# Cluster labels from one product per tile, and an issue order from a stored list of shifts

## The chip, the cores and the metric

The kernel runs on one core of a Trainium2 chip. The core has five engines that work through instruction streams of their own: TensorE (PE in the profile; its weight loads are listed apart as PEld), VectorE (DVE), ScalarE (ACT), GpSimd (POOL) and SyncE (SP), which issues all DMAs here. Semaphores order the streams; within a stream, order is fixed when the program is built. The metric is device time in microseconds, the median over runs; lower is better.

## The reference

Clustered attention, then a feed-forward block. For 4 batches, 8 heads, 768 positions and 64 dimensions per head, every query and key is given the label of the one of its head's 16 centroids with the largest cosine, and a query attends only to keys with its own label:

```
q_assign = argmax(q_n . c_n)          # per head, 16 clusters
k_assign = argmax(k_n . c_n)
scores = where(q_assign == k_assign, q . k / 8, -1e9)
attn = softmax(scores);  x = attn @ v           # 3072 rows of 512
h = x @ w_in;  g = where(h >= 1, h, where(h <= -1, 0, (h + 1)^2 / 4))
out = g @ w_out                                  # 512 -> 2048 -> 512
```

## The kernel before, in words

Inputs are float32. Each operand of a product is split into two halves in half precision (hi and lo), and products are summed over the hi and lo terms that matter. The work is cut into 8 units (`NU`): batch b and chunk c, where a chunk is 2 of the 6 position tiles of 128 per head. Heads go in pairs (hp, 4 of them).

Per batch and head pair: `kv_load`, `k_scale` (a power-of-two scale), `k_split` (hi and lo, then a transpose by DMA into `kT`), `v_split`, and `k_assign` (labels of 12 key tiles, written as a one-hot mask beside the keys). Per unit: `q_load`, `q_scale`, `q_split`, `q_assign` (labels of 16 query tiles) and `q_pairs`. Then, per unit and head pair, 4 score tiles: `at_scores` multiplies (a *score group*: 4 products with 384 columns into a PSUM tile `pair`), and VectorE evicts it (an *eviction*: `CUSTOM_DVE_ANT_0 sS<-pair`, whose accumulator read writes `sbi`); `at_soft` takes the exponential on ScalarE, splits it with ScalarE and GpSimd and transposes it by DMA; `at_av` multiplies with v into `banka` (tiles `pT`, `rr`). After each unit, `ffn1` (24 products with 256 columns into one of the banks h, i, j; then `r` on VectorE, ScalarE, VectorE; `g` on ScalarE and GpSimd) and `ffn2` (12 products with 512 columns into `pair`) run once per 256 of the 2048 hidden columns. In the first steps the weights of the feed-forward block are also brought in and split (`w`, `wk`, `word`: VectorE, ScalarE and GpSimd).

**Labels.** `labels` multiplies each transposed tile `xT[:, i]` (its 128 contraction rows hold the hi and the lo half of the 64 dimensions) with `cT[:, a]`, the 16 centroids of its head: a = 0 holds the hi half of the centroids twice, a = 1 the lo half. The two products, each a weight load and a matmul with 16 columns, accumulate in PSUM to one z of 16 columns. VectorE then takes the maximum over 16 (`mx`), compares, multiplies with `iota`, and takes the maximum again.

**Order of issue.** Nothing is issued at once. A `Recorder` keeps every instruction as a node with its predecessors (products of one `rec.group()` are one node), and `issue` decides the order. `forward` is a list scheduler: it steps through a model of the engines (`Machine`, with prices from `price`, latencies, a throttled TensorE clock) and takes on each engine the ready node with the lowest priority value. `backward` does the same from the end and gives new priorities. `issue` alternates them 80 times (`ROUNDS`), replays each order by `replay` at 4 phases of the clock window with random delays, keeps the order with the lowest sum, and then emits it. All engines' streams follow that order, so every instruction stands at the recorder's one line, and groups are told apart by tile names.

`early()` is true for steps under 22 (the first unit and a half): there, score groups alternate between the two `pair` tiles. Later ones use `pair[0]` alone, and `pair[1]` belongs to `ffn2`.

Of the kernel before, what the change touches and what calls it, by code (L numbers as in the profile page):

```python
# [34 lines left out]
WINDOW, SLOW, FULL = 3413.0, 0.41, 0.77  # L35
PHASES = (0.0, 850.0, 1700.0, 2550.0)


LATER, LATER_DMA, SLACK = 25, 600, 20

# [3 lines left out]
LOOK, MARGIN = 0.4, 4000  # L44
ROUNDS = 80

class Recorder:
# [9 lines left out]
    def __init__(self, tc):  # L59
        self.tc, self.nc = tc, tc.nc  # L60
        self.nodes, self.seen, self.open, self.step = [], {}, None, -99
        for name in ("tensor", "scalar", "vector", "gpsimd", "sync"):
            setattr(self, name, Engine(self, name, getattr(tc.nc, name)))
# [23 lines left out]
    def price(self, eng, op, out, ins, kw):  # L87
# [11 lines left out]
        if eng == "tensor":  # L99
            n = self.free(ins[1])  # L100
            half = self.free(ins[0]) <= 64 and n > 100
            if ins[1].dtype == F32:
                n *= 4

            return n / 4.8 + 3.5 if half else max(n / 2.4 + 2.5, 24)
        if eng == "scalar":
# [24 lines left out]
    def add(self, eng, op, fn, args, kw):  # L131
        outs = [kw[k] for k in ("out", "accum_out") if kw.get(k) is not None]
        pos = [a for a in args if isinstance(a, bass.AP)]
        if "out" not in kw:
            outs.insert(0, pos.pop(0))
        ins = pos + [a for k, a in kw.items() if k not in ("out", "accum_out") and isinstance(a, bass.AP)]
        node = self.open
        if node is None:
            node = Node(eng, self.step, len(self.nodes))
            self.nodes.append(node)  # L140
# [42 lines left out]
    def forward(self, prio):  # L183
# [3 lines left out]
        at = dict.fromkeys(self.nodes, 0.0)  # L187
        m = Machine(PHASES[0], slack=SLACK)
        clock = m.clock
# [46 lines left out]

    def replay(self, phase):

        m = Machine(phase, Random(int(phase)))
        left = {x: len(x.preds) for x in self.nodes}  # L240
        at = dict.fromkeys(self.nodes, 0.0)
        todo = {}
        for x in reversed(self.order):
            todo.setdefault(x.eng, []).append(x)
        while todo:
            starts = []
            for e, q in todo.items():
                x = q[-1]
                if not left[x]:
                    t = max(m.clock.get(e, 0.0), at[x])  # L250
                    starts.append((max(t, m.free(x, t)), x.i))
            t, i = min(starts)
            x = self.nodes[i]
            todo[x.eng].pop()
            if not todo[x.eng]:
                del todo[x.eng]
            self.done(x, m.run(x, t), at, left, lambda y: None)
        return m.span

    def backward(self, prio):  # L260
# [42 lines left out]
        return start  # L303

    def issue(self):
        for x in self.nodes:
            for y in x.preds:
                y.succs.append(x)
        prio = {x: x.step for x in self.nodes}
        best = None  # L310
        for _ in range(ROUNDS):
            self.forward(prio)
            starts = {x: x.start for x in self.nodes}
            span = sum(self.replay(p) for p in PHASES)
            if best is None or span < best[0]:
                best = span, self.order
            prio = self.backward(starts)
        span, self.order = best
        with self.tc.manual_schedule():
            for x in self.order:  # L320
                for fn, args, kw in x.calls:
                    fn(*args, **kw)  # L322


class Machine:


    def __init__(self, phase, noise=None, slack=0):
        self.noise, self.slack = noise and noise.random, slack
        self.clock, self.bank = {}, {}  # L330
# [15 lines left out]
    def run(self, x, t):  # L346

        e = x.eng
        if x.dma:
# [8 lines left out]
            end = self.ring + (490 if tr else 1300)  # L358
            if self.noise:
                end += LATER_DMA * self.noise()  # L360
            self.sent.append(end)
        else:
# [3 lines left out]
            end = x.busy + LATENCY[e] + self.slack  # L366
            if self.noise:
                end += LATER * self.noise()
        for k in x.banks:
# [18 lines left out]
class Node:  # L388
    def __init__(self, eng, step, i):
        self.eng, self.step, self.i = eng, step, i  # L390
        self.banks = set()
# [4 lines left out]
class Group:  # L396
# [5 lines left out]
    def __enter__(self):  # L402
        r = self.rec
        r.open = Node("tensor", r.step, len(r.nodes))
        r.nodes.append(r.open)

    def __exit__(self, *a):
        self.rec.open = None

# [38 lines left out]
def tile_clustered_attention_moe(  # L448
# [203 lines left out]

    def labels(z1, xT, n, heads):

        with rec.group():
            for i in range(n):
                for a in range(2):
                    h = heads[i]
                    rec.tensor.matmul(
                        z1[:, i], xT[:, i], cT[:, a, h * C : (h + 1) * C], start=(a == 0), stop=(a == 1)  # L660
                    )
# [9 lines left out]
        return wide(mx)  # L671

# [49 lines left out]
    def k_assign(b, hp):  # L722

        e = KV[b, hp]
        n = 2 * T
        z1 = misc(n, C)
# [540 lines left out]
    for s in sorted(ev):  # L1267
        rec.step = s
        for fn, args in ev[s]:
            fn(*args)  # L1270
    rec.issue()
# [32 lines left out]
```

## Time and profile before

| | |
|---|---|
| median of 3 runs | 867.04 us (865.24 to 868.20) |
| profiled execution, own time | 869.13 us |
| its span, first to last instruction | 867.3 us |
| TensorE busy | 809.4 us, 93% |
| VectorE busy | 650.4 us, 75% |
| ScalarE busy | 637.4 us, 73% |
| GpSimd busy | 550.1 us, 63% |
| mean granted TensorE clock | 0.984 |

The page gives each engine's busy time, the chain of work that ended last, and groups of like instructions (busy time, mean duration, idle time before them and what ended it). A matmul's duration is its whole way through the array; the next one starts long before that ends. The pace of TensorE is therefore read from starts: from the start of one group to the start of the next, divided by the number of products.

### The profile page before, as it was taken

To read this page: it belongs to the slowest core of one execution; us is meant where nothing else is said; L and a number is where in the kernel's file an instruction comes from. 1 tells how busy PE (TensorE), PEld (TensorE's weight loads), DVE (VectorE), ACT (ScalarE), POOL (GpSimd) and SP (SyncE) were. 2 spreads that over 40 slices of the span, in tenths; PEclk is the share of its full clock that TensorE was granted. 3 is DMA by queue.
4 is the path that set the end of the run, shared out by engine and by line. 5 is a ranking of instruction groups with operands and counts; after the bars stand their busy time and mean duration, and the time that the engine had idled before them with its cause. 6 is when DMAs were issued, how large, how long until landed. Compare 5 with 4: busy or idle time off the path is not lost.

```text
span 867.3 us, 19633 instructions
## 1 busy us (share of the span) xinstructions
PE 809.4 (93%) x7452; PEld 561.1 (65%) x7452; DVE 650.4 (75%) x1485; ACT 637.4 (73%) x1128; POOL 550.1 (63%) x527
## 2 busy tenths in 40 slices
PE   3687559999999999999999999999999999999997
PEld 3454346666767766767666766767667667676664
DVE  7999999998978868678778768678887757544322
ACT  6799888986867778678777687686776687676232
POOL 1166688876756777756766677666667577666222
PEclk9998889999999999999999999999999999999999
DMA  9985689869999979988998978998999787666100
GB/s 315 241 248 146 171 204 204 147 140 162 197 169 199 168 151 177 192 185 190 183 189 173 169 141 173 198 161 167 177 216 162 141 160 131 113 135 109 20 25 25
DMA packets 404767, 142.55 MB, mean 164 GB/s; under 512 B 372800, under 2 KB 396352, under 8 KB 404672
## 3 DMA queue, kind: packets, MB, share of 16 engines
q1 hardware_dynamic: 404672, 141.30, 80.2%
q8 instruction: 58, 0.95, 0.5%
q14 instruction: 37, 0.30, 0.1%
HBM read 40.40 MB, written 6.29 MB: 54 GB/s over the span
## 4 chain that ended last, share of the span: by engine, by line
PE 80%; DVE 12%; ACT 3%; issue 2%; DMA 2%; POOL 0%; ACTq 0%; SPq 0%; DVEq 0%; POOLq 0%
PE pair L322 40%; PE banka L322 11%; PE bankj L322 10%; PE banki L322 9%; PE bankh L322 9%; DVE sS L322 2%; DVE w L322 2%; DVE wk L322 1%; ACT w L322 1%; DMA q<-qn 1%; ACT hl L322 1%; DVE banki L322 1%; DVE qn L322 1%; ACT sS L322 1%; DVE q L322 1%
## 5 line engine op out<-in xcount | busy, mean ns | idle before, releaser
L322 POOL TENSOR_TENSOR hl<-sS,hl 128x768 f16<-128x768 f32 x176 | 299.8, 1711 | 116.0 <-ACT hl L322 83.7
L322 PE MATMUL pair<-w,g 128*128 128x512 f16 x1152 | 271.1, 379 | 0.0
L322 PEld LDWEIGHTS <-w 128*128 128x128 f16 x2304 | 223.4, 98 | 44.3 <-issue 2.6
L322 ACT ACTIVATE sS<-sS,sbi 128x768 f32<-128x768 f32 x192 | 179.3, 934 | 91.9 <-DVE sbi L322 88.6
L322 DVE CUSTOM_DVE_ANT_0 sS<-pair,zero,er 128x768 f32<-128x768 f32 x192 | 194.2, 1011 | 66.4 <-PE pair L322 41.6
L322 PEld LDWEIGHTS <-g 128*128 128x128 f16 x1152 | 110.3, 98 | 116.3 <-issue 1.6
L322 PE MATMUL pair<-kv,q 128*128 128x384 f16 x768 | 160.9, 334 | 17.6 <-DVE sbi L322 9.2
L322 ACT CAST hl<-sS 128x768 f16<-128x768 f32 x176 | 143.8, 825 | 12.9 <-DMA pT<-hl 7.9
L322 POOL TENSOR_TENSOR g<-r,g 128x512 f16<-128x512 f32 x88 | 103.7, 1179 | 63.7 <-ACT g L322 53.8
L322 PEld LDWEIGHTS <-q 128*128 128x128 f16 x1152 | 84.1, 99 | 72.8 <-issue 26.1
L322 PE MATMUL banka<-pT,kv 128*64 128x256 f16 (+1 forms) x1680 | 107.2, 282 | 0.4 <-DMA pT<-hl 0.4
L322 ACT ACTIVATE r<-r,f_ra,f_rs 128x512 f32<-128x512 f32 x88 | 71.3, 811 | 43.3 <-DVE r L322 42.5
L322 PEld LDWEIGHTS <-kv 128*64 128x64 f16 (+1 forms) x1968 | 96.9, 108 | 2.9 <-issue 1.5
L322 ACT CAST g<-r 128x512 f16<-128x512 f32 x88 | 53.8, 611 | 13.1 <-DVE r L322 10.2
L322 PE MATMUL bankh<-x,w 128*128 128x256 f16 x432 | 51.9, 273 | 0.2 <-POOL x L322 0.2
L322 POOL TENSOR_TENSOR qn<-qn,phi 128x256 f16<-128x256 f16 x48 | 34.2, 731 | 27.1 <-DVE phi L322 17.5
L322 PE MATMUL bankj<-x,w 128*128 128x256 f16 x408 | 48.3, 273 | 0.0
L322 PE MATMUL banki<-x,w 128*128 128x256 f16 x312 | 38.0, 273 | 0.0
L322 POOL TENSOR_TENSOR w<-w 128x1024 f16<-128x1024 f32 x12 | 30.2, 2513 | 10.6 <-ACT w L322 9.3
L322 PE MATMUL banki<-wk,w 128*128 128x256 f16 x312 | 36.7, 273 | 0.0
L322 ACT ACTIVATION_READ_ACCUMULATOR sS<-sS,sbi 128x1 f32 x192 | 36.0, 188 | 0.0
L322 PEld LDWEIGHTS <-ones 128*128 128x128 bf16 x256 | 18.0, 105 | 27.2 <-issue 21.6
(238 smaller groups left out, 1069.0 us busy)
## 6 DMA issues: line engine op xcount, KB each, us to landing
w<-in_moe_w_out_dram SPq DMA_DIRECT2D x14, 512.0 KB, 4.4
q<-in_q_dram SPq DMA_DIRECT2D x12, 512.0 KB, 4.9
kv<-in_k_dram SPq DMA_DIRECT2D x16, 384.0 KB, 3.8
kv<-in_v_dram SPq DMA_DIRECT2D x16, 384.0 KB, 4.4
out_dram<-o SPq DMA_DIRECT2D x11, 512.0 KB, 3.3
w<-in_moe_w_in_dram SPq DMA_DIRECT2D x10, 512.0 KB, 5.6
word<-in_moe_w_in_dram SPq DMA_DIRECT2D x6, 512.0 KB, 4.6
o<-in_v_dram SPq DMA_DIRECT2D x8, 384.0 KB, 4.5
```

Of the source, the lines that this page charges most:

```text
L322: fn(*args, **kw)
```

## The change

Three things change.

1. `labels`: outside `early()`, one product per tile with both halves of the centroids, `cT[:, :, h*C:(h+1)*C]`, 32 columns, into a PSUM tile twice as wide. A new `tensor_reduce` on VectorE adds the two halves into a tile in SBUF: for queries `zs`, for keys the third part of the slot, where the raw v lay. The first maximum and the comparison read that tile; the rest is as it was. Early label groups (4 of 16 for keys, 2 of 12 for queries) are unchanged.
2. Prices in `price` for products with at most 64 output rows: 3.5 ns less each, and 248 ns (`TILED`) for each group that has any; the least price of a product is 25.2 instead of 24.
3. `issue`: 59 rounds of `forward` and `backward` without `replay`; then 200 stored seeds each shift the priorities of a few recorded steps (`nudge`), and one last `forward` gives the order.

The core of the diff (the list of 200 seeds and the removed `replay` left out):

```diff
+PHASE = 0.0
...
+BASE = 59
+NUDGES = (
+    1700000017, 1700000018, 1700000028, 1700000071, 1700000073, 1700000079, 1700000104, 1700000109,
...
+)
+TILED = 248
...
-            return n / 4.8 + 3.5 if half else max(n / 2.4 + 2.5, 24)
+            self.tiled |= half
+            return n / 4.8 if half else max(n / 2.4 + 2.5, 25.2)
...
+    def nudge(self, seed, prio):
+
+        a = mix(seed * 2654435761 + 1)
+        b = mix(a + 1)
+        c = mix(b + 1)
+        names = sorted({x.ev for x in self.nodes})
+        lo, every, size = b % len(names), (1, 2, 5)[(a >> 8) % 3], float(500 << ((a >> 16) % 5))
+        at = {y: i for i, y in enumerate(names)}
+        for x in self.nodes:
+            i = at[x.ev]
+            if lo <= i < lo + (1 << (a % 8)) and not (i - lo) % every:
+                r = c if c >> 8 & 1 else mix(c + i * 7919)
+                prio[x] += ((r & 0xFFFF) / 32768.0 - 1.0) * size
...
         prio = {x: x.step for x in self.nodes}
-        best = None
-        for _ in range(ROUNDS):
+        for _ in range(BASE):
             self.forward(prio)
-            starts = {x: x.start for x in self.nodes}
-            span = sum(self.replay(p) for p in PHASES)
-            if best is None or span < best[0]:
-                best = span, self.order
-            prio = self.backward(starts)
-        span, self.order = best
+            prio = self.backward({x: x.start for x in self.nodes})
+        for seed in NUDGES:
+            self.nudge(seed, prio)
+        self.forward(prio)
...
-    def labels(z1, xT, n, heads):
-
+    def labels(xT, n, heads, tmp):
+
+        both = not early()
+        z1 = misc(n, 1 + both, C)
         with rec.group():
             for i in range(n):
+                h = heads[i]
+                if both:
+                    rec.tensor.matmul(z1[:, i], xT[:, i], cT[:, :, h * C : (h + 1) * C], start=True, stop=True)
+                    continue
...
+        zz, z1 = z1, z1[:, :, 0]
+        z = tmp if both else z1
+        if both:
+            rec.vector.tensor_reduce(out=z, in_=zz.rearrange("p n a c -> p n c a"), op=ALU.add, axis=AX.X)
...
-        rec.vector.tensor_reduce(out=mx, in_=z1, op=ALU.max, axis=AX.X)
-        rec.vector.tensor_tensor(out=z1, in0=z1, in1=wide(mx), op=ALU.is_equal)
+        rec.vector.tensor_reduce(out=mx, in_=z, op=ALU.max, axis=AX.X)
+        rec.vector.tensor_tensor(out=z1, in0=z, in1=wide(mx), op=ALU.is_equal)
...
-        mx = labels(z1, e["kT"], n, [2 * hp + i // T for i in range(n)])
+        z1, mx = labels(e["kT"], n, [2 * hp + i // T for i in range(n)], view(e["parts"][2], [n, C], F32))
...
-        z1 = misc(NQ, C)
-        mx = labels(z1, e["qT"], NQ, [i // CT for i in range(NQ)])
         zs = e["z"] = new("zs", [NQ, C], F32)
+        z1, mx = labels(e["qT"], NQ, [i // CT for i in range(NQ)], zs)
```

What it moves. On TensorE, 14,586 rows become 13,978: 608 fewer, 304 weight loads and 304 matmuls. The streams of all engines are rearranged from about the first score group on. Three places follow, in the order of the program.

VectorE, from the eviction of the 21st score group on (the rows `ISA sS_..,sbi_..` are evictions and their accumulator reads; `r` belongs to `ffn1`, `hl` to `v_split`, `word` and `wk` to the weights, `aq`'s `bankj`, `iq` and `sq` to `q_scale`), before:

```order
L322 ISA sS_85,sbi_156<-pair_79,zero,er_148 128x768
L322 ISA sbi_156 128x1
L322 SCALAR_TENSOR_TENSOR r_209<-bankj,f_gs_204,r_209 128x512
L322 SCALAR_TENSOR_TENSOR hl_172<-kv_62,sv_141,hl_172 128x768
L322 SCALAR_TENSOR_TENSOR word_71<-word_71,wk_69 128x1024
L322 ISA sS_86,sbi_157<-pair_80,zero,er_148 128x768
L322 ISA sbi_157 128x1
L322 TENSOR_SCALAR bankj<-bankj 128x4
L322 RECIPROCAL rs_160<-rs_160 128x4
L322 TENSOR_SCALAR iq_127<-bankj 128x4
L322 RECIPROCAL sq_129<-iq_127 128x4
L322 SCALAR_TENSOR_TENSOR word_71<-word_71 128x1024
```

and now, from the same eviction on:

```order
L350 ISA sS_85,sbi_156<-pair_79,zero,er_148 128x768
L350 ISA sbi_156 128x1
L350 ISA sS_86,sbi_157<-pair_80,zero,er_148 128x768
L350 ISA sbi_157 128x1
L350 TENSOR_SCALAR r_209<-bankj,f_lo_184,f_hi_179 128x512
L350 TENSOR_REDUCE v_am_125<-x_74 128x1
L350 SCALAR_TENSOR_TENSOR r_209<-bankj,f_gs_204,r_209 128x512
L350 TENSOR_SCALAR wk_69<-wk_69 128x1024
L350 TENSOR_SCALAR bankj<-bankj 128x4
L350 TENSOR_SCALAR iq_127<-bankj 128x4
L350 RECIPROCAL sq_129<-iq_127 128x4
L350 SCALAR_TENSOR_TENSOR word_71<-word_71,wk_69 128x1024
```

The row behind each piece is the eviction of the 23rd group. Before, three long operations stand between the evictions of the 21st and 22nd group and one between those of the 22nd and 23rd; now none, and five.

TensorE, between the 23rd and the 24th score group, before (`pair_79` is the tile of both groups; `bankj<-aq` is the product of `q_scale`):

```order
L322 LDWEIGHTS q_66
L322 MATMUL pair_79<-kv_62,q_66 128x384
L322 LDWEIGHTS ones
L322 MATMUL bankj<-aq_126,ones 128x4
L322 LDWEIGHTS q_66
L322 MATMUL pair_79<-kv_62,q_66 128x384
```

and now, the end of what stands there (`banki<-x` are products of `ffn1`, `bankh<-wk` those of the weights' sums):

```order
L350 LDWEIGHTS w_78
L350 MATMUL banki<-x_72,w_78 128x256
L350 LDWEIGHTS ones
L350 MATMUL bankj<-aq_126,ones 128x4
L350 LDWEIGHTS ones
L350 MATMUL bankh<-wk_69,ones 128x128
```

Before, one small product stands between the 23rd and the 24th score group; now 24 products of `ffn1` stand ahead of it and 8 of the weights' sums behind it. Those 24, and the 24 of the other half that now stand between the 22nd and the 23rd group, stood ahead of the 21st group before.

VectorE, the first label group that the change touches (queries of the third unit; `zs` receives the sum), before:

```order
L322 TENSOR_REDUCE mx_145<-banki 128x16
L322 TENSOR_TENSOR banki<-banki,mx_145 128x256
L322 ISA sS_85,sbi_158<-pair_79,zero,er_148 128x768
L322 ISA sbi_158 128x1
L322 TENSOR_SCALAR r_209<-bankh,f_lo_184,f_hi_179 128x512
L322 TENSOR_TENSOR banki<-banki,iota 128x256
L322 TENSOR_REDUCE mx_145<-banki 128x16
```

and now:

```order
L350 TENSOR_REDUCE zs_145<-banki 128x256
L350 TENSOR_REDUCE mx_146<-zs_145 128x16
L350 SCALAR_TENSOR_TENSOR r_209<-bankh,f_gs_204,r_209 128x512
L350 ISA sS_85,sbi_158<-pair_79,zero,er_148 128x768
L350 ISA sbi_158 128x1
L350 TENSOR_REDUCE v_am_125<-x_74 128x1
L350 TENSOR_TENSOR banki<-zs_145,mx_146 128x16x16
```

The new sum stands ahead of the first maximum, and the comparison reads `zs` instead of the bank.

More of the change, by code (lines that the diff above doesn't have):

```diff
@@ L2 @@
 from heapq import heapify, heappop, heappush
-from random import Random
 import concourse.bass as bass
@@ L35, with mix @@
 WINDOW, SLOW, FULL = 3413.0, 0.41, 0.77
-PHASES = (0.0, 850.0, 1700.0, 2550.0)
-LATER, LATER_DMA, SLACK = 25, 600, 20
+PHASE = 0.0
+SLACK = 20
 TURN, TURN_WAIT = dict(vector=185, gpsimd=118), 200
 LOOK, MARGIN = 0.4, 4000
-ROUNDS = 80
+BASE = 59
+NUDGES = (
[25 rows of a table added]
+)
+TILED = 248
+def mix(a):
+    a &= 0xFFFFFFFF
+    a ^= a >> 16
+    a = a * 0x7FEB352D & 0xFFFFFFFF
+    a ^= a >> 15
+    a = a * 0x846CA68B & 0xFFFFFFFF
+    return a ^ a >> 16
 class Recorder:
@@ L60, in __init__ @@
         self.tc, self.nc = tc, tc.nc
-        self.nodes, self.seen, self.open, self.step = [], {}, None, -99
+        self.nodes, self.seen, self.open, self.step, self.ev = [], {}, None, -99, 0
+        self.tiled = False
         for name in ("tensor", "scalar", "vector", "gpsimd", "sync"):
@@ L139, in add @@
             node = Node(eng, self.step, len(self.nodes))
+            node.ev = self.ev
             self.nodes.append(node)
@@ L187, in forward @@
         at = dict.fromkeys(self.nodes, 0.0)
-        m = Machine(PHASES[0], slack=SLACK)
+        m = Machine(PHASE, SLACK)
         clock = m.clock
@@ L235, in forward @@
         return m.span
[L237 to L258, printed above, removed]
     def backward(self, prio):
@@ L325, with __init__ @@
 class Machine:
-    def __init__(self, phase, noise=None, slack=0):
-        self.noise, self.slack = noise and noise.random, slack
+    def __init__(self, phase, slack):
+        self.slack = slack
         self.clock, self.bank = {}, {}
@@ L358, in run @@
             end = self.ring + (490 if tr else 1300)
-            if self.noise:
-                end += LATER_DMA * self.noise()
             self.sent.append(end)
@@ L366, in run @@
             end = x.busy + LATENCY[e] + self.slack
-            if self.noise:
-                end += LATER * self.noise()
         for k in x.banks:
@@ L389, in __init__ @@
     def __init__(self, eng, step, i):
-        self.eng, self.step, self.i = eng, step, i
+        self.eng, self.step, self.i, self.ev = eng, step, i, 0
         self.banks = set()
@@ L404, in __enter__ @@
         r.open = Node("tensor", r.step, len(r.nodes))
+        r.open.ev = r.ev
         r.nodes.append(r.open)
     def __exit__(self, *a):
-        self.rec.open = None
+        self.rec.open.cost += TILED * self.rec.tiled
+        self.rec.open, self.rec.tiled = None, False
 class Engine:
@@ L725, in k_assign @@
         n = 2 * T
-        z1 = misc(n, C)
         kn = e["kn"]
-        mx = labels(z1, e["kT"], n, [2 * hp + i // T for i in range(n)])
+        z1, mx = labels(e["kT"], n, [2 * hp + i // T for i in range(n)], view(e["parts"][2], [n, C], F32))
         rec.vector.tensor_tensor(out=z1, in0=z1, in1=mx, op=ALU.subtract)
@@ L1269, in tile_clustered_attention_moe @@
         for fn, args in ev[s]:
+            rec.ev += 1
             fn(*args)
```

5 lines of the change are left out of this document (2 added, 3 removed), and 24 rows, old and new, of the table NUDGES.

## The prediction

> **What bounds the kernel now.** I read the page's head first, then the busy times by stretch, then TensorE's waits, then the chain. The head gives span and totals:
>
> ```profile
> span 867.3 us, 19633 instructions
> PE 809.4 (93%) x7452; PEld 561.1 (65%) x7452; DVE 650.4 (75%) x1485; ACT 637.4 (73%) x1128; POOL 550.1 (63%) x527
> ```
>
> An average of 93% can hide two regimes, so the next view is busy time in stretches (length, then busy time and number of instructions of each engine, granted clock, DMA share, GB/s):
>
> ```profile
> core 0: us, PE busy (x) PEld busy (x) DVE busy (x) ACT busy (x) POOL busy (x), PEclk, DMA share, GB/s
> 0.00:40.00 40.00, 20.31 (x232) 15.54 (x233) 34.22 (x97) 29.14 (x46) 5.34 (x30) 0.96 0.92 276
> 40.00:80.00 40.00, 29.43 (x280) 19.57 (x282) 39.22 (x101) 36.64 (x58) 23.71 (x23) 0.89 0.79 214
> 80.00:120.00 40.00, 25.20 (x195) 17.22 (x192) 37.57 (x78) 35.41 (x51) 28.09 (x17) 0.88 0.65 174
> 120.00:160.00 40.00, 34.01 (x310) 23.51 (x310) 37.67 (x82) 32.29 (x58) 36.20 (x28) 0.92 0.86 188
> 160.00:200.00 40.00, 38.19 (x336) 25.58 (x335) 37.39 (x82) 36.42 (x68) 31.47 (x28) 1.00 0.82 152
> 200.00:800.00 600.00, 599.45 (x5653) 417.78 (x5652) 446.53 (x1025) 447.70 (x822) 409.97 (x391) 1.00 0.89 168
> 800.00:868.00 68.00, 62.78 (x455) 41.95 (x452) 17.77 (x24) 19.83 (x31) 15.33 (x15) 0.99 0.09 25
> ```
>
> There are two regimes. From 200 us to 800 us TensorE is busy for 599.45 of 600 us at full clock, while VectorE idles for 600 - 446.53 = 153 us. Before 200 us TensorE idles for 19.69 + 10.57 + 14.80 + 5.99 + 1.81 = 52.9 us and its clock is partly withheld, while VectorE, from 40 us to 200 us, idles for only 0.78 + 2.43 + 2.33 + 2.61 = 8.2 us. So the start is paced by VectorE, the rest by TensorE. The waits of TensorE from 200 us to the end, and the chain over the whole span, say the same:
>
> ```profile
> PE bankj L322 <- DMA q<-qn: 0.6, 1, 0.6
> ```
>
> ```profile
> PE 80%; DVE 12%; ACT 3%; issue 2%; DMA 2%; POOL 0%; ACTq 0%; SPq 0%; DVEq 0%; POOLq 0%
> ```
>
> One wait of 0.6 us in 667 us: whatever work is taken off TensorE there shortens the kernel in full, and whatever is added to VectorE there is free as long as it fits into the 153 us.
>
> **The labels on TensorE.** Of 16 key groups 4 are early, of 12 query groups 2. The change touches 12 groups of 24 products and 10 of 32: 288 + 320 = 608 products become 304. Their price, from TensorE's rows in order of time (start, duration, count; a group's pace is the distance to the next start):
>
> ```profile
> 136.79 0.95 PE L322 MATMUL banki<-cT,q 128*128 128x16 f16 x32 [0.64 <-DVE r L322]
> ...
> 203.29 0.96 PE L322 MATMUL bankj<-cT,q 128*128 128x16 f16 x32 [0.55 <-DMA q<-qn]
> ...
> 244.93 0.30 PE L322 MATMUL banki<-n,ones 128*128 128x32 f16 x6
> 245.09 1.46 PE L322 MATMUL pair<-w,g 128*128 128x512 f16 x6
> ...
> 254.00 2.78 PE L322 MATMUL bankj<-x,w 128*128 128x256 f16 x24
> 256.62 0.75 PE L322 MATMUL bankh<-cT,kv 128*128 128x16 f16 x24
> 257.23 0.81 PE L322 MATMUL pair<-kv,q 128*128 128x384 f16 x4
> ```
>
> A label group of 24 takes 257.23 - 256.62 = 0.61 us, 25.4 ns per pair of load and matmul with 16 columns. The nearest row with 32 columns is `banki<-n,ones`: 0.16 us for 6, 26.7 ns. So doubling the columns costs nothing or 1.3 ns. Saved: 608 x 25.4 - 304 x 26.7 = 7.3 us, or 304 x 25.4 = 7.7 us if 32 columns pass as fast as 16. I take **7.5 us**. The first touched group is that at 136.79 us, the next that at 203.29 us, so all but the first (16 x 25 ns, 0.4 us) lie where TensorE is the bound.
>
> The rule that would change this sum is one on the pace of small products. The Trainium skill, "TensorE: Matmul & The Clock Gate", section "Back-to-back issue gap", says that in a stream of weight loads and matmuls both set the pace, and gives some 81 ns per pair for 128 columns; with that as an estimate for each of the 304 pairs the labels would bring 24.6 us. Its table in the same section has an issue floor of about 25 ns for 1 to 64 columns, and it is this that the trace agrees with (25.4 and 26.7 ns).
>
> **The labels on VectorE.** 22 new sums read 512 (queries) or 384 (keys) values from PSUM. No row has this, so I extend the maxima over the same bank, and look at what the comparison costs once both its inputs lie in SBUF (instruction, shapes, count; busy time, mean ns):
>
> ```profile
> L322 DVE TENSOR_REDUCE mx<-banki 128x12 f32<-128x192 f32 x12 | 4.2, 351 | 2.0 <-PE banki L322 1.8
> L322 DVE TENSOR_REDUCE mx<-bankh 128x16 f32<-128x256 f32 x10 | 4.2, 417 | 0.8 <-PE bankh L322 0.7
> L322 DVE TENSOR_TENSOR banki<-zs,has 128x256 f32<-128x256 f32 x4 | 3.0, 756 | 0.0
> L322 DVE TENSOR_TENSOR bankh<-bankh,mx 128x256 f32<-128x256 f32 x5 | 2.1, 428 | 0.1
> ```
>
> 66 ns for 64 values is 1.03 ns each: 417 + 264 = 681 ns for a query sum, 351 + 198 = 549 ns for a key sum, 10 x 0.68 + 12 x 0.55 = 13.4 us in all. The comparison reads two SBUF tiles; the nearest such row is 756 ns against 428 ns now, so at most 22 x 0.33 = 7.3 us more, at least nothing. Of these 13.4 to 20.7 us, one query group falls into the part before 200 us (cost 0.7 us, counted); the others lie in the part with 153 us of idle VectorE time, and I cost them at nothing. If that cover were gone, they would cost 13.4 us (second rival). They also make a label some 0.6 us late. The new sum waits for the product that the old maximum waited for, so it adds no wait on another engine's result; behind it on VectorE are evictions, for which TensorE waits, and these it delays by its own 0.55 to 0.68 us. The sum of a key group is written where the raw v lay, but the last reader of that, the second half of `v_split`, stands on VectorE itself.
>
> **The order.** After 200 us TensorE has nothing left to gain but 0.6 us. At the end it runs without a gap into the last products in both orders, the last `ffn1` group of 24 ahead of 36 products of `ffn2`. So the order can gain only before 200 us, and only what VectorE idles there, 8.2 us, for the score groups keep their place among VectorE's rows within a few. The longest wait of the start after the first loads shows what is at stake, on TensorE and then on VectorE:
>
> ```profile
> 113.66 0.81 PE L322 MATMUL pair<-kv,q 128*128 128x384 f16 x4
> 115.21 0.81 PE L322 MATMUL pair<-kv,q 128*128 128x384 f16 x4 [0.74 <-DVE sbi L322]
> 115.87 0.16 PE L322 MATMUL bankj<-aq,ones 128*128 128x4 bf16 x1
> 121.77 1.44 PE L322 MATMUL pair<-kv,q 128*128 128x384 f16 x4 [5.73 <-DVE sbi L322]
> ```
>
> ```profile
> 114.15 1.00 DVE L322 CUSTOM_DVE_ANT_0 sS<-pair,zero,er 128x768 f32<-128x768 f32 x1
> ...
> 115.75 1.30 DVE L322 SCALAR_TENSOR_TENSOR hl<-kv,sv,hl 128x768 f16<-128x768 f32 x1
> 116.98 1.21 DVE L322 SCALAR_TENSOR_TENSOR word<-word,wk 128x1024 uint32<-128x1024 uint32 x1
> 118.11 1.00 DVE L322 CUSTOM_DVE_ANT_0 sS<-pair,zero,er 128x768 f32<-128x768 f32 x1
> ...
> 120.70 1.00 DVE L322 CUSTOM_DVE_ANT_0 sS<-pair,zero,er 128x768 f32<-128x768 f32 x1
> 121.64 0.08 DVE L322 DVE_READ_ACCUMULATOR2_ANT sbi<- 128x1 f32 x1
> ```
>
> The 24th score group waits 5.73 us for the eviction of the 23rd from the same tile, behind `r`, `hl` and `word`. In the new order 24 products of `ffn1` stand between the two (2.62 us, from 254.00 to 256.62 above), so TensorE fills part of it. But VectorE was busy in that wait, and its own work stays; what counts is only its idle time, 2.43 us in 80:120. I take **2.4 us** for the order: that one stretch's idle time gone, of 8.2 us at most; at the other end nothing, or a loss (first rival).
>
> **Sum.** 7.5 + 2.4 - 0.7 = 9.2 us. The profiled execution took 869.13 us, 1.8 us over its span, so it would take 859.9 us; the median of 867.04 us lies 2.1 us lower, and becomes **857.8 us**. About 0.3% (2.6 us, 864.4 to 869.6) is what a measurement of this kernel can tell from no change.
>
> **The rivals.**
>
> *The new order starts worse (20%).* A list of shifts fitted to the model's durations may put an instruction at the head of VectorE's or ScalarE's stream that on the chip is not ready, and all behind it waits. For it: in the start VectorE and ScalarE are both over 80% busy from 40 us on, and the granted clock of 0.88 to 0.92 shows how uneven TensorE's feed is there; a row of the same kind cost 5.73 us. Against it: the groups stand in much the same order as before, and VectorE's rows move by a few places. The Trainium skill, "TensorE: Matmul & The Clock Gate", section "What's actually happening", has the clock's windows run free of the kernel's start, which an order fitted to one phase would not suit; a single profile can't show it. Time: 867.04 - 7.5 + 0.7 = 860.2 us with no gain from the order, 866.0 us with one more wait of 5.73 us.
>
> *The sums on VectorE land on the path (4%, slower).* If VectorE, not TensorE, set the pace behind 200 us, the 22 sums would cost 13.4 us against the labels' 7.5 us: 867.04 + 5.9 = 872.9 us. It decides from the point at which over 10.1 of the 13.4 us are late for TensorE. Against it: 153 us of idle VectorE time and 0.6 us of waits.
>
> *The labels bring nothing (3%).* A product with 32 columns would have to cost twice one with 16. Against it: 26.7 ns. Time: 867.04 - 2.4 + 0.7 = 865.3 us.
>
> *The weight loads are not hidden (1%).* A load lasts 99 ns in its group:
>
> ```profile
> L322 PEld LDWEIGHTS <-q 128*128 128x128 f16 x1152 | 84.1, 99 | 72.8 <-issue 26.1 <-DVE q L322 2.4 <-DMA q<-qn 0.8
> ```
>
> If each pair cost that, 304 fewer would bring 30.1 us, and 835.2 us. Against it: the 24 pairs in 0.61 us.
>
> *The order gains more than VectorE idles (2%)*: under 851 us. It would take shorter VectorE operations in the start, and nothing in the change shortens them.
>
> **How the numbers follow.** My forecast (70%) spans 867.04 - 7.7 - 8.2 = 851.1 us to 860.2 us, its likeliest value 857.8 us. Widened by the spread of the three runs (1.5 us) below, and into the first rival above, the range is 849.5 to 863.5 us. Faster by over 0.3%: the forecast, the case of more gain, the loads and most of the first rival, 90%. Within 0.3%: the labels without effect and the rest of the first rival, 6%. Slower: 4%.
>
> **What would show it.** Right: a label group of 12 or 16 at 25 to 27 ns per product; sums of 0.5 to 0.8 us; still under 2 us of TensorE waits behind 200 us; TensorE idle before 200 us at 48 to 53 us. Wrong: waits for `mx`, `zs` or `sbi` on TensorE behind 200 us, or an idle time before 200 us that moved by over 8 us either way.

## The result and the profile after

The changed kernel takes 863.34 us (median of 8 runs, 859.18 to 864.68) against 867.91 us (865.24 to 870.10) for the kernel before, run in turn with it. The ratio is 0.9939 [0.9919, 0.9958], so it is 5.3 us faster (3.6 to 7.0); the plain difference of the two medians, 4.6 us, lies inside that interval. The profiled execution is one of the fastest: 860.89 us. Its head, and the busy times in the stretches used before (columns as there):

```profile
span 859.1 us, 19058 instructions
PE 802.4 (93%) x7148; PEld 555.1 (65%) x7148; DVE 652.3 (76%) x1507; ACT 639.1 (74%) x1128; POOL 548.3 (64%) x527
```

```profile
0.00:40.00 40.00, 19.22 (x209) 15.01 (x210) 34.11 (x97) 29.48 (x47) 4.33 (x29) 0.97 0.92 279
40.00:80.00 40.00, 29.74 (x299) 22.01 (x298) 39.12 (x100) 37.08 (x56) 21.27 (x18) 0.86 0.79 211
80.00:120.00 40.00, 25.72 (x206) 17.35 (x203) 39.23 (x82) 37.38 (x58) 36.28 (x26) 0.91 0.72 191
120.00:160.00 40.00, 38.02 (x329) 25.45 (x329) 37.76 (x88) 32.14 (x56) 29.75 (x26) 0.96 0.98 192
160.00:200.00 40.00, 38.44 (x353) 26.20 (x354) 35.80 (x84) 37.87 (x70) 35.61 (x30) 1.00 0.88 160
200.00:800.00 600.00, 596.69 (x5376) 412.99 (x5374) 450.28 (x1040) 447.80 (x820) 408.87 (x390) 1.00 0.89 167
```

Before 200 us TensorE idles for 20.78 + 10.26 + 14.28 + 1.98 + 1.56 = 48.9 us, 4.0 us less than before. From 200 us to 800 us it idles for 3.3 us, 2.8 us more than before. TensorE's waits behind 200 us have grown. The one for `q<-qn` was there before (0.6 us); the other three groups are new, and all are for VectorE:

```profile
PE bankj L350 <- DVE r L350: 1.0, 2, 0.6
PE bankj L350 <- DMA q<-qn: 1.0, 1, 1.0
PE bankj L350 <- DVE has L350: 0.8, 1, 0.8
PE pair L350 <- DVE sbi L350: 0.5, 1, 0.5
```

TensorE's rows show the long wait of the start cut from 5.73 to 2.90 us, and a touched label group: 16 products with 32 columns from 467.21 to 467.63 us, 0.42 us or 26 ns each.

```profile
119.74 1.44 PE L350 MATMUL pair<-kv,q 128*128 128x384 f16 x4 [2.90 <-DVE sbi L350]
...
467.21 0.57 PE L350 MATMUL bankj<-cT,q 128*128 128x32 f16 x16 [0.95 <-DMA q<-qn]
467.63 0.81 PE L350 MATMUL pair<-kv,q 128*128 128x384 f16 x4
```

The idle time of VectorE from 40 us to 200 us is 0.88 + 0.77 + 2.24 + 4.20 = 8.1 us, as before (8.2 us).

On VectorE the sums have the predicted length; the comparison, which now reads two SBUF tiles, varies:

```profile
L350 DVE TENSOR_REDUCE zs<-banki 128x256 f32<-128x512 f32 x4 | 2.7, 682 | 0.0
L350 DVE TENSOR_REDUCE kv<-bankh 128x192 f32<-128x384 f32 x4 | 2.2, 551 | 0.0
L350 DVE TENSOR_TENSOR bankh<-zs,mx 128x256 f32<-128x256 f32 x3 | 2.5, 834 | 0.0
L350 DVE TENSOR_TENSOR bankj<-kv,mx 128x192 f32<-128x192 f32 x4 | 1.5, 366 | 0.1
```

In the two profiled executions the span falls by 8.2 us: TensorE is busy 7.0 us less (809.4 to 802.4), and idles 1.2 us less. The medians differ by less, since the profiled execution of before lay 1.2 us above its median and that of after 2.5 us below.

### The profile page after: what moved, and what is told of

Same layout as the page of the kernel before. It is cut to its first block, busy times and chain, and to the rows that moved or that the text cites. A ratio compares the mean times of both kernels' runs of the same rounds, so it can differ in the third digit from the quotient of the medians.

```text
span 859.1 us, 19058 instructions
## 1 busy us (share of the span) xinstructions
PE 802.4 (93%) x7148; PEld 555.1 (65%) x7148; DVE 652.3 (76%) x1507; ACT 639.1 (74%) x1128; POOL 548.3 (64%) x527
## 4 chain that ended last, share of the span: by engine, by line
PE 71%; DVE 9%; issue 3%; ACT 3%; POOL 3%; DMA 2%; ACTq 0%; DVEq 0%; POOLq 0%
PE pair L350 35%; PE banka L350 10%; PE banki L350 9%; PE bankj L350 9%; PE bankh L350 8%; DVE sS L350 2%; DVE r L350 2%; DMA q<-qn 1%; POOL hl L350 1%; ACT sS L350 1%; DVE qn L350 1%; DMA pT<-hl 1%; ACT hl L350 1%; DVE w L350 1%; DVE banki L350 0%
## 5 line engine op out<-in xcount | busy, mean ns | idle before, releaser
L350 PE MATMUL pair<-kv,q 128*128 128x384 f16 x768 | 158.3, 329 | 17.1 <-ACT pT L350 8.5
L350 POOL TENSOR_TENSOR g<-r,g 128x512 f16<-128x512 f32 x88 | 106.4, 1209 | 74.3 <-ACT g L350 64.1
L350 PEld LDWEIGHTS <-q 128*128 128x128 f16 x992 | 78.7, 98 | 72.3 <-issue 25.5
L350 PEld LDWEIGHTS <-kv 128*64 128x64 f16 (+1 forms) x1824 | 92.4, 108 | 4.0 <-ACT kv L350 1.4
L350 DVE TENSOR_SCALAR r<-bankh,f_lo,f_hi 128x512 f32<-128x512 f32 x30 | 24.2, 805 | 13.7 <-PE bankh L350 10.9
```

## The experiments

All orders but two (those of the run without shifts and of the run with before's planner) are replayed: `issue` no longer plans, but emits a stored list of instructions. So the labels and the order, which the change alters together, can be taken apart. Ratios are to the kernel before, run on the same chip; microseconds are the ratio's distance from 1 times 867.9 us, unless two kernels of one chip are compared by their medians. The diffs show the lines that matter; for a replayed list they say in words what changed in it.

```diff
-        for _ in range(BASE):
-            self.forward(prio)
-            prio = self.backward({x: x.start for x in self.nodes})
-        for seed in NUDGES:
-            self.nudge(seed, prio)
-        self.forward(prio)
+        raw = zlib.decompress(base64.b64decode(ORDER))
+        for k in array.array("h", raw):
...
+        for x in want:
+            late.append(x)
```

An instruction whose inputs stand later in the list is held back until they are out.

**The new labels in before's order.** The list is that of before, each sum directly ahead of the maximum that reads it; the sums of keys go to a tile of their own, and four half groups of `ffn1` move back.

```diff
-        z = tmp if both else z1
+        z = (tmp if n == NQ else new("zt", [n, C], F32)) if both else z1
```

> The new labels (one product per tile, sum on VectorE) in the order of before, each sum right ahead of its first maximum; key sums in a tile of their own, and four half groups of ffn1 moved back behind a label that now fills their bank. Theory A (the labels bring their 7.5 us in any order; the new order wins some 5 us before 200 us and loses some 4.5 us to waits behind it): ratio to before 0.991 to 0.993, TensorE waits behind 200 us under 2 us. Theory B (the waits behind 200 us come from the labels themselves, their sums and wider banks): ratio 0.995 to 0.998, with 3 us or more of TensorE waits behind 200 us.

Measured: 889.06 us, ratio 1.0244 [1.0223, 1.0265], 21.2 us slower. No theory had that. The stretch behind 200 us, and TensorE's waits there:

```profile
200.00:800.00 600.00, 578.58 (x5189) 397.11 (x5188) 459.59 (x1027) 432.13 (x796) 397.31 (x379) 0.99 0.86 164
```

```profile
PE pair L321 <- DVE sbi L321: 9.1, 9, 1.7
PE bankh L321 <- DVE zs L321: 3.7, 1, 3.7
PE banki L321 <- DVE zs L321: 2.7, 1, 2.7
PE bankj L321 <- DVE zs L321: 1.3, 1, 1.3
```

TensorE idles 21.4 us where it idled 0.55 us, while VectorE still idles for 140 us. The waits are for evictions (`sbi`) and for banks that VectorE frees late (`zs`, the last step of a query label).

**The old labels in the new order.** After's list without its sums, two products per tile; against the kernel of the first experiment one switch differs besides the list.

```diff
-NEW, SUMS = True, 1
+NEW, SUMS = False, 1
```

> The old labels (two products per tile, no sum) in the order of after, everything else as in after. Theory A: the order by itself is worth about nothing, 5 us won and 4.5 us lost: ratio to before 0.998 to 1.003, with the waits of after still there behind 200 us. Theory B: without the sums the waits behind 200 us go, the start stays: ratio 0.993 to 0.996.

Measured: 869.26 us, 1.0017 [1.0006, 1.0029], 1.5 us slower. By itself the order brings nothing, as theory A has it: TensorE's idle time before 200 us is 48.8 us, as in after, but behind 200 us it is 3.1 us instead of 0.55 us. These idle times don't account for the 1.5 us, though: they fall by 1.6 us in all, and the profiled span is 1.0 us shorter than that of before (866.3 against 867.3 us). The loss shows in the medians alone, and its cause stays open.

**The start of the one, the rest of the other.** The same new labels, with two mixed lists, joined at about 200 us; only the list differs from that of the first experiment.

```diff
-ORDER = (the list of before)
+ORDER = (the list of after up to 200 us, then that of before; and the other way round)
```

> The new labels; the order of after up to the 41st eviction, then all that is left in the order of before. Theory A: the gain of the start without the loss behind it: 7.5 + 5 = 12.5 us, ratio 0.985 to 0.988, TensorE waits behind 200 us under 2 us. Theory B: the loss stays with the labels: ratio 0.991 to 0.994.

> The new labels; the order of before up to the 41st eviction, then all that is left in the order of after. Theory A: the labels' 7.5 us less the 4.5 us that the later part of the new order loses: ratio 0.995 to 0.998, TensorE idle 52 to 54 us before 200 us. Theory B: the same as the labels in the old order, 0.995 to 0.998; this run alone does not part the two, it does so with the third.

Measured: 887.50 us, 1.0216 [1.0191, 1.0241], with the new start and the old rest; 872.43 us, 1.0064 [1.0044, 1.0084], with the old start and the new rest. Both miss. The waits of the first experiment stay with the old rest (`sbi` 8.2 us, `zs` 8.1 us): it is the rest of before's order, not its start, that can't take the sums. The second has a wait of 2.0 us at the joint that neither parent has, so how much of its 5.6 us is the old start stays open.

**The sum alone, and the wide bank alone, in before's order.** Two products per tile as before. The first sums each value with itself, which leaves the labels as they are; the second only takes the bank twice as wide, without a sum (the four half groups of `ffn1` move back here too).

```diff
+        late = not early()
+        both = False
...
+            rec.vector.tensor_reduce(out=z, in_=z1.unsqueeze(3).to_broadcast([P, n, C, 2]), op=ALU.add, axis=AX.X)
```

```diff
+        z1 = misc(n, 1 if early() else 2, C)
```

> The order of before and its two products per tile into half a bank; added is only a sum on VectorE of the size of the new one (it adds z to itself, so labels stay the same), right ahead of the first maximum. The labels in the old order lost 21 us where 7.5 us should have been won, some 28 us in all. Theory C1 (the sums do it: VectorE's row is longer by 0.55 to 0.68 us 22 times, evictions behind come late, TensorE waits): ratio to before 1.015 to 1.03. Theory C2 (the full banks do it: the sums fit into VectorE's idle time): ratio 0.999 to 1.005.

> The order of before and its two products per tile, no sum, but the results spread over a bank twice as wide, so that nothing else fits into the bank until the label is done; the same four half groups of ffn1 move back behind a label. Theory C1: ratio to before 0.999 to 1.005. Theory C2: ratio 1.015 to 1.03, with TensorE waiting for the label's last steps on VectorE.

Measured: 882.48 us, 1.0177 [1.0157, 1.0196], 15.4 us slower, for the sums; 869.78 us, 1.0030 [1.0018, 1.0042], 2.6 us slower, for the bank: theory C1. Here a wait can be followed row by row. VectorE, around one turn from eviction to eviction, in the kernel before and then with the sums:

```profile
395.51 0.43 DVE L322 TENSOR_TENSOR banki<-banki,mx 128x256 f32<-128x256 f32 x1
...
397.96 1.01 DVE L322 CUSTOM_DVE_ANT_0 sS<-pair,zero,er 128x768 f32<-128x768 f32 x1
...
399.82 0.35 DVE L322 TENSOR_TENSOR bankj<-bankj,mx 128x192 f32<-128x192 f32 x1
...
401.79 0.69 DVE L322 SCALAR_TENSOR_TENSOR bankj<-ik,iq 128x1 f32<-128x1 f32 x1
402.80 1.02 DVE L322 CUSTOM_DVE_ANT_0 sS<-pair,zero,er 128x768 f32<-128x768 f32 x1 [0.32 <-PE pair L322]
```

```profile
398.15 0.68 DVE L321 TENSOR_REDUCE zs<-banki 128x256 f32<-128x512 f32 x1
...
400.13 1.88 DVE L321 TENSOR_TENSOR banki<-zs,mx 128x256 f32<-128x256 f32 x1
...
404.03 1.01 DVE L321 CUSTOM_DVE_ANT_0 sS<-pair,zero,er 128x768 f32<-128x768 f32 x1
...
404.96 0.55 DVE L321 TENSOR_REDUCE zt<-bankj 128x192 f32<-128x384 f32 x1
...
406.48 1.16 DVE L321 TENSOR_TENSOR bankj<-zt,mx 128x192 f32<-128x192 f32 x1
...
409.26 1.01 DVE L321 SCALAR_TENSOR_TENSOR bankj<-ik,iq 128x1 f32<-128x1 f32 x1
410.18 1.00 DVE L321 CUSTOM_DVE_ANT_0 sS<-pair,zero,er 128x768 f32<-128x768 f32 x1
```

And TensorE's score group ahead of the second of these evictions and the next one, which needs the tile that this eviction empties, before and with the sums:

```profile
401.83 0.82 PE L322 MATMUL pair<-kv,q 128*128 128x384 f16 x4
...
405.26 0.81 PE L322 MATMUL pair<-kv,q 128*128 128x384 f16 x4
```

```profile
406.11 0.82 PE L321 MATMUL pair<-kv,q 128*128 128x384 f16 x4
...
411.25 0.81 PE L321 MATMUL pair<-kv,q 128*128 128x384 f16 x4 [1.56 <-DVE sbi L321]
```

Before, 4.84 us lie between the two evictions, and VectorE waits 0.32 us for TensorE at their end. With the sum it is 6.15 us, 1.3 us more: 0.55 us for the sum, 0.81 us for the slower comparison and 0.32 us for a small operation (`bankj<-ik,iq`), less the 0.32 us of waiting. But VectorE comes into this turn late already. TensorE's score group stands 4.3 us later than before (406.11 against 401.83 us), the first eviction 6.1 us: 1.8 us late, behind a query label whose comparison took 1.88 instead of 0.43 us, and whose sum took 0.68 us. The second eviction is then 3.1 us late. TensorE waits 1.56 us and not 3.1 us, since before the tile was empty at 403.82 us (402.80 + 1.02) and TensorE came to it at 405.26 us.

So the room of a turn has two parts: what VectorE waits in it (here 0.32 us), and how far ahead of TensorE's need it is done (here 1.4 us). The 153 us that VectorE idles in all don't count; only what lies in this turn does. And the lateness comes more from the two longer comparisons (1.45 and 0.81 us) than from the two sums (0.68 and 0.55 us). Over the kernel VectorE is busy 22.1 us longer (650.4 to 672.4), some 13.5 us of it sums and 7.7 us comparisons, and 15.4 us come out at the end. How much of these is owed to each this run doesn't tell.

**After without its shifts.** `NUDGES` is empty; 59 rounds of the planner set the order.

```diff
-NUDGES = (
...
-)
+NUDGES = ()
```

> The kernel after with an empty list of seeds: 59 rounds of forward and backward on the new labels and prices, no shifts. If the stored shifts are what wins the start (theory A, an order worth 5 us there): ratio to before 0.998 to 1.010, TensorE idle 52 to 60 us before 200 us. If any order planned with the new labels does as well, and the shifts add nothing that the chip shows: ratio 0.992 to 0.996.

**Before's planner with the new labels.** Before's program, prices and 80 rounds with replay, with only `labels` and its two callers changed.

```diff
-    def labels(z1, xT, n, heads):
+    def labels(xT, n, heads, tmp):
```

> The kernel before with the new labels alone, planned anew by the planner of before (80 rounds, replay at 4 phases, old prices). Theory A as it stands after the first runs (the labels bring their 7.5 us in any order that was planned with them): ratio to before 0.989 to 0.995. Rival: the planner of before has no order without waits for the fuller banks and the sums, and the shifts were needed: ratio 0.998 to 1.008.

Measured: 872.25 us, 1.0056 [1.0040, 1.0071], without the shifts; 874.83 us, 1.0090 [1.0072, 1.0108], with the old planner. So the labels alone, even with an order that before's planner made for them, make this kernel 7.8 us slower, somewhat more than the rival of that expectation has it. Without the shifts after would be 4.9 us slower than before, so the shifts are worth some 9 to 10 us. Both lose in the start and behind it: TensorE idles 56.5 and 56.0 us before 200 us, and 7.6 and 6.5 us from there to 800 us. VectorE is busy 681.0 and 665.8 us there, against 652.3 us in after, with the same 1507 instructions; the 22 comparisons behind the sums take 18.1 and 16.2 us against 11.6 us. So the list with its shifts holds the sums in part because other operations of VectorE are shorter in it.

**Each sum twice, in after's order.**

```diff
-NEW, SUMS = True, 1
+NEW, SUMS = True, 2
...
                     for _ in range(SUMS if x.sums else 1):
                         fn(*args, **kw)
```

> The kernel after with each of the 22 sums issued twice in a row (13.4 us more on VectorE, same results, same order). Theory D (no order has slack for them: VectorE's idle time is spent waiting inside a loop with TensorE, so the added time falls on the path in this order as it did in the old one): 13 us more than after, ratio to before 1.007 to 1.012. Theory E (the searched order made room for the sums, with something to spare): at most 4 us more than after, ratio 0.994 to 0.998.

Measured: 878.11 us, 1.0123 [1.0102, 1.0144]. Against after on the same chip (below) that is 14.7 us, for 13.6 us of added sums; VectorE is busy 18.5 us longer in all (656.3 to 674.8 us), since other operations get longer too. Theory D has it nearly (1.007 to 1.012), theory E is out. The stretch behind 200 us shows where: TensorE idles 14.2 us, VectorE 133 us.

```profile
200.00:800.00 600.00, 585.76 (x5247) 402.74 (x5245) 466.59 (x1056) 441.95 (x810) 400.60 (x386) 1.00 0.86 165
```

The longest of TensorE's waits there:

```profile
PE banki L322 <- DVE n L322: 3.1, 4, 1.9
PE banki L322 <- DVE zs L322: 1.6, 1, 1.6
```

Waits for the last step of a label (`n` for keys, `zs` for queries) make up 7.6 us, those for evictions under 0.2 us. So in this order the added time does not come out at the `pair` tile, but at the banks and masks for which TensorE waits until a label is done.

So the new order has no spare room on VectorE either; it holds the 22 sums that it was planned with, and not 22 more.

**The late waits moved, and after again.** Five groups on TensorE are moved behind one or two others, so that what they waited for is ready; the second kernel is after, replayed.

```diff
-... label group of 16 (467 us), score group, 12 products of ffn1 ...
+... score group, 12 products of ffn1, label group of 16 ...
```

> The kernel after with five groups on TensorE set one or two places back, behind work that is ready (ahead of them, 12 label products, a score group and 12 products of ffn1, 12 products of ffn1, and one at_av), at four of the five places where it waits longest behind 200 us (252, 466, 474 and 647 us). If these waits are what the new order loses: 3 us less than after, ratio to before 0.989 to 0.992. If the wait only moves to what is late next: ratio as after, 0.992 to 0.996.

> The program of after once more, its order given as a list, to stand beside the other three on one chip. All theories: ratio to before 0.992 to 0.996.

Measured: 862.11 us, 0.9936 [0.9919, 0.9953], with the waits moved; 863.40 us, 0.9950 [0.9934, 0.9965], for after again, as in the first comparison. The 1.3 us between them are within the spread. TensorE still idles 4.3 us from 200 to 800 us; the waits are for other things now:

```profile
PE pair L322 <- DVE sbi L322: 1.6, 3, 0.9
PE bankh L322 <- DMA kv<-n: 1.2, 1, 1.2
PE bankj L322 <- DVE zs L322: 1.0, 1, 1.0
PE bankj L322 <- DVE r L322: 0.4, 1, 0.4
```

So the waits move on; a version that beats after for certain was not found.

**Two products and the sum, in after's order.** After's list with all its sums, which again add each value to itself, and two products per tile.

```diff
-        both = not early()
+        late = not early()
+        both = False
...
+            rec.vector.tensor_reduce(out=z, in_=z1.unsqueeze(3).to_broadcast([P, n, C, 2]), op=ALU.add, axis=AX.X)
```

> The order of after with its sums on VectorE, but two products per tile into half a bank again (the sum adds z to itself): what after has without what it saves on TensorE. If 304 products are worth 7.5 us there: 7 to 8 us more than after. With the sums free in this order it is the same as the run with old labels in this order, ratio to before 1.000 to 1.003; if the sums cost 4 us or more there: ratio 1.005 to 1.010.

Measured: 868.39 us, 1.0006 [0.9993, 1.0019]. After again, with half the products, is 5.0 us faster; 7 to 8 us were expected. The same order without any sum (1.0017) is not faster than with them: in after's order the sums cost nothing, in before's 15.4 us. The rows are those of after again and of this kernel:

```profile
200.00:800.00 600.00, 596.12 (x5365) 411.83 (x5363) 454.16 (x1045) 449.22 (x824) 410.69 (x393) 1.00 0.89 167
```

```profile
200.00:800.00 600.00, 597.30 (x5607) 415.69 (x5605) 453.07 (x1043) 447.55 (x819) 407.61 (x389) 1.00 0.89 167
```

From 200 us to 800 us TensorE idles 3.9 us with one product, 2.7 us with two.

## Why the prediction was right, and where it was not

The forecast was faster by 9.2 us; it is faster, by 5.3 us, and the time of 863.34 us lies 0.2 us under the upper end of the range, 3.1 us above the band of the forecast itself. That is the band of the first rival ("the new order starts worse"), though not by its mechanism: the start got better, and the loss lay behind it. The single steps:

**Labels on TensorE: the size of the work was right, its worth too high.** The pace is 26 ns per product as forecast. The Trainium skill, "TensorE: Matmul & The Clock Gate", section "Back-to-back issue gap", has some 81 ns per pair for 128 columns and, in its table, an issue floor of about 25 ns for 1 to 64 columns; this pace agrees with the floor. With the order held fixed TensorE's busy time falls by 7.3 us (815.4 us with two products and the sum, 808.1 us in after again) against the 7.5 us of the prediction. The time falls by 5.0 us. In the two profiles, whose spans differ by 5.3 us, the other 2.0 us are idle time of TensorE: 1.2 us the waits behind 200 us just shown, as if TensorE got to VectorE's work sooner and waited there for part of what it saved, and 0.8 us before 200 us, where two runs of one program differ by more than that (48.9 us of idle time in after, 47.0 us in after again). "Whatever work is taken off TensorE there shortens the kernel in full" was too much.

**Sums on VectorE: the size right, the reason why they cost nothing wrong.** They take 0.55 and 0.68 us as extrapolated, and the comparisons behind them 11.6 us where they took 8.6 us, within the 7.3 us more that the prediction allowed. It costed all this at nothing since "whatever is added to VectorE there is free as long as it fits into the 153 us", although it saw that the sums delay evictions and make a label late. Three runs refute that: in before's order the sums and their slower comparisons cost 15.4 us, twice the sums in after's order cost 14.7 us, and with before's planner the whole label change costs 7.8 us. Of the orders that ran, only after's, which the stored shifts made, and its variant with five groups moved are faster with the new labels than the kernel before. The idle 153 us were read as room; they are the waits of an engine that works in turn with others. The profile of before showed that it does, in a view that the prediction did not use, VectorE's own waits between 200 and 800 us:

```profile
DVE sS L322 <- PE pair L322: 41.4, 43, 2.3
DVE r L322 <- ACT r L322: 19.4, 26, 1.8
DVE rs L322 <- ACT rs L322: 14.2, 11, 2.9
DVE sS L322 <- POOL hl L322: 9.0, 8, 2.3
```

The largest is the wait of the evictions for the score group, and the score group in turn needs the tile that the eviction before has emptied. An operation that comes between the two delays TensorE once it exceeds the wait of that one turn and the time by which the tile is empty ahead of need. The label banks work alike: TensorE can't use such a bank again, or the mask of the keys, before the label's last step is done, and in the run with doubled sums it is these that it waits for. The second rival, "the sums on VectorE land on the path", was given 4% and 872.9 us. Before's planner with the new labels measured 874.8 us, in the direction of that rival. That the numbers lie so close is partly chance: of TensorE's added idle time there, 3.2 us lie before 200 us and 5.9 us behind it, and TensorE still is the busier engine behind 200 us.

**Order: the gain of the start was there, and was given back.** TensorE's idle time before 200 us fell from 52.9 to 48.9 us, within the 48 to 53 us forecast, and the 5.73 us wait to 2.90 us. Where the gain came from was wrong: the prediction priced it by VectorE's idle time ("only what VectorE idles there"), but VectorE idles as long as before from 40 us to 200 us (8.1 us). And the step "so the order can gain only before 200 us", with 2.4 us for it, failed: it did not see that the order can also lose behind 200 us, where there was only 0.6 us to gain. 2.8 us of new waits arose there (3.3 us of waits in all; "still under 2 us" was the forecast, and waits for `sbi`, 0.5 us here, were to show that it was wrong). With the old labels the order costs 1.5 us, where a gain of 2.4 us was forecast.

The terms as measured on one chip, then (a plus is slower): order and sums together +0.5 us (two products and the sum), the products -5.0 us, in all -4.5 us, where -9.2 us was forecast; the first comparison gave -5.3 us (3.6 to 7.0). That the time lies inside the range is in part luck. The sums came out free as forecast, but only in the new list; the labels brought 5.0 us and not 7.5 us, the order nothing and not 2.4 us; and the range reached up to such a time only for the sake of a rival whose mechanism was another. Taken one at a time the parts are worth +7.8 us (labels, with before's planner) and +1.5 us (order), both slower.

Open are: the 15.4 us of the sums alone and the 2.6 us of the wide bank make 18.0 us, but the new labels in before's order cost 21.2 us, although they save TensorE 7 us (the comparisons took 18.3 us there against 16.3 us with the sums alone, which is part of it); why the old labels lose 1.5 us in the new order; and how much of the loss of the new labels in before's order comes from the length of the sums and how much from the comparisons.

## What to carry to other kernels

Idle time of an engine that works in turn with the bound one is not room: before costing an operation on it at nothing, read how long it waits in the very turn where the operation goes, and how far ahead of need its result is there (0.32 and 1.4 us in the turn shown). Work that is moved from the bound engine to its partner needs an order planned with it, and the two can be worth something only together; replaying a stored order with one part undone at a time shows which part is worth what. Where a list of searched shifts carries the gain (9 to 10 us here, of a gain of 5), it is fitted to this program, and any later edit puts it at risk.

## What the runs showed of the hardware

The comparison of a query group has one shape, but with both inputs in SBUF it took between 0.42 and 1.92 us in the run with the sums alone. There the one at 400.13 us (shown with the experiment, 1.88 us) stands beside these GpSimd rows:

```profile
400.07 1.65 POOL L321 TENSOR_TENSOR hl<-sS,hl 128x768 f16<-128x768 f32 x1
401.65 0.59 POOL L321 MEMSET n<- 128x576 f16 x1
```

Of the 22 comparisons of after, those beside which GpSimd had nothing to do took 0.35 to 0.43 us, and every one above 0.6 us had a GpSimd operation beside it for at least three quarters of its time. With the input in PSUM, in the kernel before, all 56 operations of this kind (the comparisons and the subtractions of the labels) took 0.34 to 0.43 us, those with GpSimd busy beside them throughout too. The Trainium skill, "SBUF — State Buffer", section "SBUF: two separate sides", says that VectorE and GpSimd share a pair of ports as a lock, that an operation of VectorE with two inputs in SBUF contends for it with one of GpSimd that reads SBUF, and that the one that starts first holds it for its whole length. The traces agree to 0.01 us: the comparison at 400.13 us ends 0.29 us after the GpSimd operation that was running when it began (1.88 against 1.59 us). In the two runs, every comparison above 0.5 us ended 0.29 us (queries) or 0.22 us (keys) after such a GpSimd operation, while one of after that began 0.01 us ahead of its GpSimd neighbour (at 720.76 us) took 0.43 us. So the same VectorE work has another length in another order: 48 operations with two inputs in SBUF, first in before, then in the kernel with the old labels in the new order:

```profile
L322 DVE SCALAR_TENSOR_TENSOR qn<-q,sq,qn 128x256 f16<-128x256 f32 x48 | 30.4, 665 | 2.9 <-ACT qn L322 2.8
```

```profile
L322 DVE SCALAR_TENSOR_TENSOR qn<-q,sq,qn 128x256 f16<-128x256 f32 x48 | 25.4, 566 | 2.4 <-ACT qn L322 2.4
```

With the same instructions VectorE was busy 650.4 us in the one and 642.3 us in the other. That is part of the room in which the new order puts the sums: after has 13.5 us of sums more than before, and VectorE is busy only 1.9 us longer. Of these 48 operations, 27 had a GpSimd operation beside them in before, 814 ns on average, and 16 in the other order, 742 ns; those without one took 466 to 486 ns in both. Whether the comparisons would stay short with the sums written to PSUM was not run.

The other thing is the spread from run to run. After again took 865.19 us in its profiled execution, 4.3 us more than after's; TensorE's granted clock from 40 to 120 us was 0.75 and 0.82, against 0.86 and 0.91 above, and its busy time there 58.7 us against 55.5 us.
